# Six loads of short rows against one load of long rows, for gate weights in an attention and expert kernel

## The chip, the cores and the metric

The kernel runs on one core of a Trainium2 chip. The metric is the device time of one execution in microseconds. Each timed run also records its span (first to last instruction, about 1.7 us less than the time) and the mean clock granted to TensorE. Some executions fall into a slower state: 310 to 315 us at a granted clock of 0.977 to 0.984. They are left out of every comparison here; each median below is that of the fast runs. Each kernel has one profiled execution per run, so the times within a profile are those of one execution.

## The reference, cut to what matters

```python
# a gated recurrence over 768 steps gives x, 3072 rows of 384; then a dense mixture of 4 experts:
p = domain_probs / (domain_probs.sum(-1, keepdims=True) + 1e-09)   # (3072, 4), float32
for e in range(4):
    h = np.maximum(x @ w1[e], 0.0)          # 384 -> 1024
    out += p[:, e:e + 1] * (h @ w2[e])      # 1024 -> 384
```

A row of `domain_probs` is four numbers, 16 bytes. The whole array is 48 KB, beside 36 MB that the kernel moves in all.

## The kernel before

The sequence is cut into 6 chunks of 128 steps. Chunk c's attention is computed while chunk c-1's experts run. A small list scheduler in the kernel, with assumed costs for every step, fixes the order of all engines at build time; the parts below are `Op`s of that plan. `rooms` are buffers, and `ps_m` holds the four PSUM banks of the expert products.

```python
pt = const.tile([128, B * C, E], FP32)       # raw probabilities, 384 bytes per partition
pn = const.tile([128, B * C, E], FP32)       # normalised
psm = const.tile([128, B * C, 1], FP32)
w1_sb = wpool.tile([128, E, KD, F], BF16)    # every later tile lies behind these constants
...
def load_w(i, e, which):                     # weights, cast to bf16 on the way, from GpSimd
    ins["w", i] = nc.gpsimd.dma_start(out=w[:, e], in_=r[e])
    if i == 0:
        after(ins["w", 0], ins[0, "k", B - 1])      # not before the last k of chunk 0 has landed
...
def load_p(c):                               # 512 rows of 16 bytes
    nc.sync.dma_start(out=p_dst[:, :, c], in_=p_src[:, :, c])
def probs(c):                                # sum, + 1e-9, reciprocal, product: four small VectorE steps
    ...
def ev_o(c, e, nt, part, cols, eng):         # out += p * (h @ w2), out of PSUM
    pe = pn[:, nt * C + c, e:e + 1]
    ...
# loads of chunk 0, from SyncE, each 192 KB as 1,024 rows of 192 bytes:
for i, x in enumerate("f0 k0 q0 f1 k1 q1 f2 f3 k2 q2 v0 k3 q3 v1 v2 v3".split()):
    add_load(0, x[0], int(x[1]), 1, -1000 + i)
...
for c in range(C):
    pl = P.add(f"ld p{c}", {"DMA": 0.5}, ..., -900 if c == 0 else u0 - 6, lag=2.0)
    pdone.append(P.add(f"probs {c}", {"DVE": 0.8}, ..., u0 + 4, deps=[pl, xdone[c, B - 1]]))
...
for o in done:                               # emission; o.pad filler matmuls keep TensorE busy at the start
    for _ in range(o.pad):
        nc.tensor.matmul(out=spare[:, 0:256], lhsT=busy[:, 0:128], rhs=busy, start=True, stop=True)
    o.emit(o.engine)
```

## Time and profile before

| kernel before | |
|---|---|
| time, median of the first 3 runs | 303.41 us (302.98 to 304.57) |
| profiled execution | 304.22 us, span 302.5 us |
| TensorE busy | 97% |
| first expert matmul to last matmul's end ("the body") | 23.83 to 299.42: 275.59 us |
| last matmul's end to the end of the span ("the end") | 3.10 us |
| the six probability loads, issue to landing | 2.1 to 7.2 us, median 2.7 |

I split the span into three parts throughout: the start up to the first expert matmul (`x @ w1`), the body, and the end. TensorE is the limit in the body; the start is a chain through loads and all engines.

### The profile page before, as it was taken

Reading aid. Unit: us, or ns where it says so; the run is one execution under the profiler, and the core shown is the slowest. Engines: PE = TensorE matmul, PEld = TensorE weight load, DVE = VectorE, ACT = ScalarE, POOL = GpSimd, SP = SyncE. Lnnn points to the kernel's source line nnn. Section 1 sums busy time; section 2 is a strip of 40 time slices with the busy share of each in tenths; the row PEclk is TensorE's granted clock in tenths of the full one; section 3 lists DMA queues with packets and bytes.
Section 4 is the critical chain, followed back from the end, with each engine's and each line's share of the span. In section 5 each row is a group of like instructions: output and inputs, shape, how many; then the busy total and the mean of one; then the engine's idle time right before and its main releaser. Section 6 shows DMA issues by size and latency. Waiting matters only on the chain.

```text
span 302.5 us, 5544 instructions
## 1 busy us (share of the span) xinstructions
PE 294.6 (97%) x2141; PEld 170.9 (56%) x2141; DVE 136.8 (45%) x269; ACT 172.1 (57%) x299; POOL 95.7 (32%) x157
## 2 busy tenths in 40 slices
PE   7898999999999999999999999999999999999995
PEld 5664555566775566556555555555556555555553
DVE  6693002789753574526364426364315253201223
ACT  5766664857776464677455575435566444475440
POOL 4584300407666047332434252622342100000000
PEclk9999999999999999999999999999999999999999
DMA  8999999963995559967799978200422201100003
GB/s 159 206 175 207 208 207 196 218 100 61 216 217 113 113 110 186 179 137 152 141 175 160 220 167 154 50 15 13 115 62 52 48 13 32 66 21 2 0 0 106
DMA packets 137355, 36.10 MB, mean 119 GB/s; under 512 B 128496, under 2 KB 135792, under 8 KB 137328
## 3 DMA queue, kind: packets, MB, share of 16 engines
q1 hardware_dynamic: 131568, 29.45, 49.8%
q0 software_dynamic: 5760, 6.29, 12.5%
q8 instruction: 17, 0.28, 0.4%
q14 instruction: 10, 0.08, 0.1%
HBM read 31.51 MB, written 4.72 MB: 120 GB/s over the span
## 4 chain that ended last, share of the span: by engine, by line
PE 90%; DMA 4%; DVE 3%; POOL 1%; ACT 1%; issue 1%; DVEq 0%; ACTq 0%; POOLq 0%
PE ps_m L356 40%; PE ps_m L344 40%; DMA w_sb<-in_moe_w_dram 3%; PE ps_t L300 2%; PE ps_t L255 1%; PE ps_t L315 1%; PE ps_t L321 1%; PE ps_t L311 1%; POOL qk L276 1%; DMA f<-in_f_logit_dram 1%; DVE qk L276 1%; PE ps_m L569 1%; PE ps_t L285 1%; DVE AT L304 0%; POOL Sf L335 0%
## 5 line engine op out<-in xcount | busy, mean ns | idle before, releaser
L344 PE MATMUL ps_m<-xT,w_sb 128*128 128x512 bf16 (+1 forms) x624 | 153.1, 363 | 1.3 <-DMA w_sb<-in_moe_w_dram 0.9
L356 PE MATMUL ps_m<-w_sb,h 128*128 128x384 bf16 x776 | 153.2, 324 | 0.0
L352 ACT ACTIVATE h<-ps_m 128x512 bf16<-128x512 f32 (+1 forms) x169 | 97.3, 577 | 98.0 <-PE ps_m L344 93.8
L356 PEld LDWEIGHTS <-h 128*128 128x128 bf16 x776 | 73.5, 98 | 58.6
L363 DVE SCALAR_TENSOR_TENSOR o<-ps_m,pn,o 128x384 f32<-128x384 f32 (+1 forms) x73 | 44.6, 611 | 107.2 <-PE ps_m L356 101.3
L344 PEld LDWEIGHTS <-w_sb 128*128 128x128 bf16 x624 | 59.5, 98 | 47.7 <-DMA w_sb<-in_moe_w_dram 1.1
L276 POOL TENSOR_TENSOR qk<-q,e 128x384 bf16<-128x384 f32 x18 | 21.6, 1204 | 64.3 <-ACT e L262 63.9
L350 DVE TENSOR_SCALAR h<-ps_m 128x512 bf16<-128x512 f32 (+1 forms) x39 | 21.9, 578 | 27.1 <-PE ps_m L344 24.2
L304 DVE TENSOR_TENSOR AT<-ps_t,mask 128x512 bf16<-128x512 f32 x48 | 30.2, 682 | 7.4 <-PE ps_t L300 7.4
L335 POOL TENSOR_TENSOR Sf<-Sf,egs 48x192 f32<-48x192 f32 x40 | 20.7, 517 | 39.9 <-DVE Sf L328 37.8
L276 POOL TENSOR_TENSOR qk<-k,e 128x384 bf16<-128x384 f32 x21 | 22.2, 1059 | 20.2 <-ACT e L264 12.9
L262 ACT ACTIVATE e<-ps_t 128x384 f32<-128x384 f32 x24 | 20.7, 864 | 4.8 <-PE ps_t L255 2.6
L328 DVE TENSOR_TENSOR Sf<-Sf,ps_t 48x192 f32<-48x192 f32 x40 | 14.0, 350 | 10.8 <-PE ps_t L321 10.0
L365 ACT ACTIVATE o<-ps_m,pn 128x384 f32<-128x384 f32 x20 | 11.6, 580 | 5.8 <-PE ps_m L356 4.3
L336 POOL CAST sb<-Sf 48x192 bf16<-48x192 f32 x40 | 13.6, 339 | 2.6
L569 PE MATMUL ps_m<-busy 128*128 128x256 bf16 x69 | 12.8, 333 | 1.3 <-DVE busy L140 1.3
L218 POOL CAST vb<-v 128x384 bf16<-128x384 f32 x18 | 9.7, 558 | 11.9 <-DMA v<-in_v_dram 9.7
L264 ACT ACTIVATE e<-ps_t 128x384 f32<-128x384 f32 x24 | 13.0, 541 | 0.0
L247 ACT ACTIVATE ex<-f 128x768 f32<-128x768 f32 (+1 forms) x14 | 10.5, 748 | 3.2 <-DMA f<-in_f_logit_dram 3.2
L315 PE MATMUL ps_t<-vb,AT 128*128 128x48 bf16 x192 | 11.4, 184 | 0.7 <-DVE vb L218 0.7
L315 PEld LDWEIGHTS <-AT 128*128 128x128 bf16 x192 | 9.8, 97 | 2.5 <-issue 0.9
L251 ACT ACTIVATE gp<-ex 128x768 bf16<-128x768 f32 (+1 forms) x14 | 10.5, 751 | 0.4
(50 smaller groups left out, 141.7 us busy)
## 6 DMA issues: line engine op xcount, KB each, us to landing
w_sb<-in_moe_w_dram POOLq DMA_DIRECT2D x8, 768.0 KB, 19.2
out_dram<-o SPq DMA_DIRECT2D x23, 192.0 KB, 2.1
f<-in_f_logit_dram SPq DMA_DIRECT2D x10, 384.0 KB, 4.2
k<-in_k_dram SPq DMA_DIRECT2D x10, 384.0 KB, 5.3
q<-in_q_dram SPq DMA_DIRECT2D x10, 384.0 KB, 5.3
v<-in_v_dram SPq DMA_DIRECT2D x10, 384.0 KB, 5.5
f<-in_f_logit_dram SPq DMA_DIRECT2D x4, 192.0 KB, 3.8
k<-in_k_dram SPq DMA_DIRECT2D x4, 192.0 KB, 4.0
```

What stands on the lines that cost most here:

```text
L262: nc.scalar.activation(out=e[:, 0].rearrange("t (d h) -> t h d", d=D), in_=cs[:, 0:HD].rearrange("t (i r d) -> t r i d", r=2, d=D), func=A ...
L276: engines[eng].tensor_tensor(out=tl("qk", c, b)[:, j, :, 0:D].rearrange("t (i r) d -> t i r d", r=2), in0=tl("qk"[j], c, b // 2)[:, hh(b), ...
L304: nc.vector.tensor_tensor(out=tl("AT", c, b)[:, r].rearrange("s i t -> s (i t)"), in0=tl("A", c, b, r).rearrange("s i t -> s (i t)"), in1= ...
L315: nc.tensor.matmul(out=y[:, h * D:(h + 1) * D], lhsT=AT[:, r, i, :], rhs=vb[:, h, :], start=(c == 0), stop=True, skip_group_check=True)
L328: nc.vector.tensor_tensor(out=Sf[rows, b], in0=Sf[rows, b], in1=KV[rows, :, r, :], op=ALU.add)
L335: nc.gpsimd.tensor_tensor(out=Sf[rows, b], in0=Sf[rows, b], in1=eg, op=ALU.mult)
L344: nc.tensor.matmul(out=tl("hp", c, e, fc, n0)[:, n0:n1], lhsT=w1_sb[:, e, kk, fc * 128:(fc + 1) * 128], rhs=tl("xT", c)[:, kk, n0:n1], sta ...
L350: nc.vector.tensor_relu(out=dst, in_=src)
L352: nc.scalar.activation(out=dst, in_=src, func=AF.Relu)
L356: nc.tensor.matmul(out=tl("op", c, e, nt, part)[:, cols], lhsT=tl("h", c, e)[:, fc, nt * T:(nt + 1) * T], rhs=w2_sb[:, e, fc, cols], start ...
L363: nc.vector.scalar_tensor_tensor(out=o, in0=op, scalar=pe, in1=o, op0=ALU.mult, op1=ALU.add)
L569: nc.tensor.matmul(out=spare[:, 0:256], lhsT=busy[:, 0:128], rhs=busy, start=True, stop=True)
```

## The change

The intent is to take six small loads off SyncE's queue, to keep the first from standing in front of the weights, to normalise once, and so to free VectorE. The array is read as 24 rows of 2,048 bytes; each expert's column of it is turned by TensorE into PSUM.

```diff
-    pt = const.tile([128, B * C, E], FP32)
-    pn = const.tile([128, B * C, E], FP32)
-    psm = const.tile([128, B * C, 1], FP32)
+    NR = B * C
+    praw = const.tile([NR, T, E], FP32)
+    ident32 = const.tile([NR, NR], FP32)
+    nc.vector.tensor_copy(out=ident32, in_=ident[0:NR, 0:NR])
+    pn = const.tile([T, E, NR], FP32)
+    psm = const.tile([T, NR], FP32)
...
-        nc.sync.dma_start(out=p_dst[:, :, c], in_=p_src[:, :, c])
+    def load_p():
+        nc.scalar.dma_start(out=praw, in_=moe_domain_probs.rearrange("(r p) e -> r p e", p=T))
+    def pe_pp():
+        for e in range(E):
+            nc.tensor.transpose(out=tl("pp")[:, e], in_=praw[:, :, e], identity=ident32)
+    def probs():   # the same four steps, once, for all 24 columns
...
-        pe = pn[:, nt * C + c, e:e + 1]
+        pe = pn[:, e, nt * C + c:nt * C + c + 1]
...
-            at = P.add(f"at {c}.{bs[-1]}", {"PE": 0.4 if len(bs) == 1 else 0.66}, ...
+            at = P.add(f"at {c}.{bs[-1]}", {"PE": 0.43 if len(bs) == 1 else 0.66}, ...
...
+    pl = P.add("ld p", {"ACT": 0.1}, lambda e: load_p(), -1100, lag=3.0)
+    pp = P.add("pp", {"PE": 0.6}, lambda e: pe_pp(), -1, deps=[pl], takes=[("ps_m", "pp")], lag=0.2)
+    pdone = P.add("probs", {"DVE": 0.9}, lambda e: probs(), 4, deps=[pp, xdone[0, B - 1]], frees=[("ps_m", "pp")])
```

## The prediction

> **What bounds the kernel now.** I read the page first (busy shares, the 40 slices, the chain that ended last), then the chain in order of time, then the timeline of the two places where the chain leaves the matmuls, and last the windows around the first probability load.
>
> ```profile
> span 302.5 us, 5544 instructions
> PE 294.6 (97%) x2141; PEld 170.9 (56%) x2141; DVE 136.8 (45%) x269; ACT 172.1 (57%) x299; POOL 95.7 (32%) x157
> PE   7898999999999999999999999999999999999995
> PE 90%; DMA 4%; DVE 3%; POOL 1%; ACT 1%; issue 1%; DVEq 0%; ACTq 0%; POOLq 0%
> ```
>
> TensorE is busy 97% of the span, and 90% of the chain that ended last is TensorE. I checked that this is real work and not waiting counted as busy: the matmuls from the first expert layer at 23.83 us to the end at 299.4 us stream 646,464 columns in all, and 512 columns take 0.215 us from start to start in an undisturbed stretch (the three at 24.49, 24.71 and 24.92 us). That is 271 us of 275.5. So after the start at most some 4 to 6 us can be won by any means, and the gaps above 0.25 us add up to 1.25 us only, all between 71 and 83 us. The probabilities are a side branch: six small loads, and four tiny VectorE operations for each of six chunks. They can matter only where they touch the chain of waits. I find two such places.
>
> The first is the start. The chain, in order of time, with start, length and what:
>
> ```profile
> 5.60 2.58 PE ps_m L569 x12
> 13.58 1.31 POOL qk L276
> 14.89 8.90 DMA w_sb<-in_moe_w_dram
> 23.83 1.47 PE ps_m L344 x6
> ```
>
> The expert work cannot start before the first weight load lands. That load is issued at 14.89 us, when GpSimd has finished its third product. TensorE's filler matmuls (L569, which keep it warm) stand on that chain, 12 of them at 5.6 us. The first probability load is issued at 14.79 us, just ahead of the weights. In the timeline and in the windows of that stretch (the last columns of the windows are clock, DMA share and GB/s):
>
> ```profile
> 14.79 0.93 SPq L237 DMA_DIRECT2D pt<-in_moe_domain_probs_dram  x1
> 14.89 6.83 POOL L229 DMA_DIRECT2D w_sb<-in_moe_w_dram  x8
> ...
> 17.00:17.50 0.50, 0.50 (x12) 0.39 (x12) 0.50 (x1) 0.47 (x2) 0.50 (x2) 1.00 1.21 88
> 17.50:18.00 0.50, 0.49 (x13) 0.35 (x8) 0.50 (x3) 0.00 (x0) 0.50 (x1) 1.00 0.92 55
> ...
> 23.00:24.00 1.00, 0.17 (x1) 0.11 (x2) 0.00 (x0) 0.00 (x0) 0.00 (x0) 1.00 1.16 219
> ```
>
> Where the 512 packets of 16 B lie among the first weight packets the rate is 88 and 55 GB/s, against 219 later. TensorE waits for the weights at the end:
>
> ```profile
> 23.83 0.98 PEld L344 LDWEIGHTS <-w_sb 128*128 128x128 bf16 x6 [1.13 <-DMA w_sb<-in_moe_w_dram]
> ```
>
> The second place is chunk 1's normalisation, which stands in VectorE's order directly ahead of two evictions that TensorE waits for:
>
> ```profile
> 81.95 0.20 DVE L244 TENSOR_TENSOR pn<-pt,psm 128x16 f32<-128x16 f32 x1
> 82.18 1.14 DVE L367 TENSOR_SCALAR o<-ps_m,pn 128x384 f32<-128x384 f32 x2
> 82.86 3.37 PE L344 MATMUL ps_m<-xT,w_sb 128*128 128x256 bf16 x27 [0.34 <-DVE o L367]
> ```
>
> **What the Trainium skill says.** DMA: Bandwidth & Descriptors, section "Why small descriptors are slow (HBM only)": each packet pays a fixed overhead, and each operation carries 32 bytes of descriptor beside its data. The trace agrees in kind: alone, a probability load moves its 8 KB in about half a microsecond of packets (a median of 2.7 us from issue to landing), a rate near 16 GB/s. Same page, "Queues, rings and completion order": SP and ACT each own one row on the same 16 DMA engines, which take turns between rows by packet. So moving the load to ACT's queue saves it a place in SP's line but gives no bandwidth of its own; the kernel before issues nothing from ACT, so its trace cannot show that. TensorE: Matmul & The Clock Gate, "What's actually happening" and "Part 4: PE-mode transpose": the array runs at half rate until about 3.4 us of sustained activity, and transposes do not count as activity in the same way. The trace agrees with the first: the 12 fillers at 5.46 us take 2.72 us (0.22 us apart), five at 20.09 us take 0.71 us (0.11 us apart), so the array was cold until after 8 us. No line here shows the second.
>
> **The change part by part.** *Removed loads.* Six issues of about 0.6 us on SyncE's queue (0.93 for the first) and 3,072 packets of 16 B. Five of them land amid work whose waits do not end on them, so they are worth nothing. The first lies ahead of the weights: 512 packets at 9 to 22 ns each over 16 engines is 0.3 to 0.7 us of DMA time, call it 0.5. The rest of the slow stretch I take to be the weight queue's own beginning, because the first 2,048 B packets take 800 ns against 173 later; that is a choice. The weights can win at most 0.8 us for TensorE: the last transposed input is copied from 22.47 for 0.48 us, and the last fillers end at 22.98, so matmuls cannot start before about 23.05.
>
> *Added load.* One issue from ACT right behind the table load (0.80 + 1.28 us = 2.1 us). ACT waits for f until 3.71 us, so the issue is hidden. 24 rows of 2,048 B are 48 KB, at 200 GB/s 0.24 us of DMA, shared with the loads of q, k and f. With 0.6 us of issue and the 2.1 to 2.7 us of the small loads it lands at about 4.8 us.
>
> *Added transposes.* They stand on TensorE behind the first cumulative sums (L255 and L258, which end at 5.4 to 5.6 us), so a landing at 4.8 is in time. The build order shows four 128x24 transposes in place of three of the 12 fillers, 69 becoming 66. Three cold fillers are 3 x 0.22 = 0.65 us. There is no fp32 matmul in this trace; the cold bf16 transposes stand about 0.12 us apart (four in 0.63 us, less the 0.27 us that one takes), and I allow one to one and a half of that each, 0.5 to 0.7 us: even. At most 0.4 us could be won, because the transposes of q at 7.98 us wait for the fillers and not for q, ready at 7.38.
>
> *VectorE.* Six times (0.17 + 0.33 + 0.18 + 0.18 us), 5.1 us in all, become one set over 96 elements in PSUM at 22 us, where VectorE then has nothing to do until 25.5. By the slope of the PSUM copies (0.56 us for 384 elements) it is about 0.25 + 0.19 + 0.20 + 0.26 = 0.9 us. VectorE's total falls by some 4 us. Only chunk 1's 0.83 us (81.32 to 82.15) lies on the path. TensorE's lost time at 82.9 and 83.4 us is 0.51 + 0.20 us above the streaming rate, so that is the most that this can return.
>
> *Moved work.* The plan of the kernel is made anew. From the first expert layer on the order of all engines differs, other buffers of the matmul room are taken, VectorE takes an eviction of QK in chunk 1 and gives others to ACT, and the 0.47 and 0.27 us that TensorE loses at 71.2 and 73.3 us, waiting for products on VectorE, may grow or go. I count this as 0, plus or minus 0.8 us.
>
> Sum: start -0.4 (weights -0.5, fillers 0, a little for a later warm-up +0.1), chunk 1 -0.5, the rest 0: -0.9 us before discount. As new orders tend to bring a wait of their own, I take 0.7, so 303.4 - 0.7 = 302.7 us.
>
> **The rivals.** (1) *The new load becomes a wait.* TensorE takes its instructions in order, so if the probabilities land at 7 us instead of 4.8, everything behind stops. For it: the six loads ahead fill the DMA (214 GB/s from 5 to 10 us), and the first small load took 7.2 us to land behind others. Against: it is on another row of the same engines, and is only 24 packets. It would also keep the array cold for another 3.4 us. This costs 0.5 to 1.5 us at the start: 303.5 to 304.5. (2) *The weights do not come earlier*, because the 55 GB/s are their own start. Then only chunk 1 is left: about 302.9 to 303.1. (3) *The new order loses more than it wins* between 66 and 90 us, the one stretch where VectorE, ACT and GpSimd are all busy over 75% (10.78, 9.91 and 9.96 of 13 us in the window of 70 to 83): plus 1 us, about 304. (4) *All goes well*: start -0.8, chunk 1 -0.7, the waits at 71 and 73 us gone, -0.7: 301.2.
>
> **Range and chances.** The rivals run from 301.2 to 304.5 with most weight on small gains; three runs of the kernel before already span 302.98 to 304.57. 8 in 10: 301.3 to 304.0. A change of 2% is 6.1 us. To be that much faster, all loss after the start would have to vanish; to be slower by that, a wait longer than any in this trace would have to appear. Faster 0.01, within 2% 0.98, slower 0.01.
>
> **What would show it.** Right: first expert matmul between 23.1 and 23.6 us; the windows at 17 to 18 us well above 88 and 55 GB/s; 66 fillers; no wait of TensorE for the probabilities; one set of small operations on VectorE, its total near 132.7 us; the wait near 82.9 us gone; TensorE busy 97% still. Wrong: a TensorE idle ended by the probability load near 5.4 us, fillers still 0.22 us apart after 10 us, the first expert matmul at or after 23.9 us, or new gaps above 0.25 us that add up to more than 1.25 us.

## The result, and the profile after

The changed kernel took 303.90 us in the median of 5 fast runs (303.51 to 304.42; a sixth run was slow, 314.16), the kernel before 303.55 us in 6 runs beside it. The ratio is 1.0012, with a 95% interval of 0.9989 to 1.0035. Ratios here are the mean time of one kernel's fast runs over that of the other's of the same rounds, so they are not quite the ratio of the medians quoted. The time lies inside the predicted range, at its upper edge, on the other side of "before" than predicted.

From the page of the changed kernel, the span, the busy shares and the chain that ended last:

```profile
span 302.7 us, 5502 instructions
PE 291.0 (96%) x2111; PEld 169.8 (56%) x2142; DVE 131.4 (43%) x248; ACT 172.4 (57%) x300; POOL 96.5 (32%) x158
PE 90%; SPq 4%; DMA 2%; issue 1%; DVE 1%; ACT 0%; DVEq 0%
```

VectorE fell by 5.4 us, as intended. TensorE's 3.6 us less are not a saving: 31 matmul records are missing from this trace (593 of 624 on the line of the first expert layer). What is new is 4% of the chain on SyncE's queue, the issues of the first loads. The same part of the chain, in order of time (start, length, what), where before the weights stood:

```profile
14.57 6.62 DMA v<-in_v_dram
...
22.54 0.34 PE ps_t L344 x3
...
24.64 0.38 PE ps_m L348
```

The start is now bound by the last v load: it landed at 21.19 us, against 17.93 before. The timeline adds what waited for loads (idle time and its cause in brackets):

```profile
0.83 0.63 ACTq L238 DMA_DIRECT2D praw<-in_moe_domain_probs_dram  x1
...
5.44 0.66 PE L242 MATMUL ps_m<-ident,praw 24*128 24x24 f32 x4
...
15.23 6.78 POOL L232 DMA_DIRECT2D w_sb<-in_moe_w_dram  x8 [0.46 <-DMA k<-in_k_dram]
...
21.21 0.51 ACT L219 CAST vb<-v 128x384 bf16<-128x384 f32 x1 [2.27 <-DMA v<-in_v_dram]
```

The new load did all that was asked of it. It was issued during the table load, its packets were through by 2.2 us, and the four transposes ran at 5.44 us without a wait. But k and v came late, so GpSimd issued the weights 0.34 us later than before. And v, still in the queue when the weights began, was overtaken: after 18.0 us its last 104 rows of 192 bytes were served beside weight packets of 2,048 bytes, one now and then, until 20.65 us.

| profiled execution | start | body | end | span |
|---|---|---|---|---|
| before | 23.83 | 275.59 | 3.10 | 302.52 |
| after | 24.64 | 274.59 | 3.48 | 302.71 |

So a gain of 1.0 us in the body stands against losses of 0.8 at the start and 0.38 at the end. The experiments are about where each of these comes from.

### The profile page after: what moved, and what is told of

It reads as the page before. It is cut to its first block, busy times and chain, and to the rows that moved or that the text cites. A ratio compares the mean times of both kernels' runs of the same rounds, so it can differ in the third digit from the quotient of the medians.

```text
span 302.7 us, 5502 instructions
## 1 busy us (share of the span) xinstructions
PE 291.0 (96%) x2111; PEld 169.8 (56%) x2142; DVE 131.4 (43%) x248; ACT 172.4 (57%) x300; POOL 96.5 (32%) x158
## 4 chain that ended last, share of the span: by engine, by line
PE 90%; SPq 4%; DMA 2%; issue 1%; DVE 1%; ACT 0%; DVEq 0%
PE ps_m L360 41%; PE ps_m L348 40%; SPq L225 4%; DMA v<-in_v_dram 2%; PE ps_t L304 2%; PE ps_t L319 1%; PE ps_t L325 1%; PE ps_t L315 1%; PE ps_t L259 1%; PE ps_t L289 1%; DVE qk L280 1%; PE ps_t L344 0%; DVE yb L221 0%; PE ps_m L573 0%; ACT xT L219 0%
## 5 line engine op out<-in xcount | busy, mean ns | idle before, releaser
L348 PE MATMUL ps_m<-xT,w_sb 128*128 128x512 bf16 (+1 forms) x593 | 149.9, 362 | 1.5 <-issue 0.2
L354 DVE TENSOR_SCALAR h<-ps_m 128x512 bf16<-128x512 f32 (+1 forms) x37 | 20.9, 581 | 28.3 <-PE ps_m L348 27.0
L266 ACT ACTIVATE e<-ps_t 128x384 f32<-128x384 f32 x24 | 20.8, 865 | 5.2 <-PE ps_t L259 3.2
L369 ACT ACTIVATE o<-ps_m,pn 128x384 f32<-128x384 f32 x22 | 12.8, 581 | 4.8 <-PE ps_m L360 4.1
L573 PE MATMUL ps_m<-busy 128*128 128x256 bf16 x66 | 11.0, 304 | 1.3 <-DVE busy L140 1.3
```

The source lines that it names most:

```text
L266: nc.scalar.activation(out=e[:, 0].rearrange("t (d h) -> t h d", d=D), in_=cs[:, 0:HD].rearrange("t (i r d) -> t r i d", r=2, d=D), func=A ...
L348: nc.tensor.matmul(out=tl("hp", c, e, fc, n0)[:, n0:n1], lhsT=w1_sb[:, e, kk, fc * 128:(fc + 1) * 128], rhs=tl("xT", c)[:, kk, n0:n1], sta ...
L354: nc.vector.tensor_relu(out=dst, in_=src)
```

## The experiments

Twelve runs were made, on three chips. All results were correct.

### The changed kernel again

No edit.

> The changed kernel, unchanged. In its first profile the first expert matmul came at 24.64 us and the last v load landed at 21.19 us, against 23.83 and 17.93 in the kernel before. Theory A (order of transfers): the late v is built in, because the first weight load is now issued only 0.66 us after that v load's issue (0.99 before) and overtakes it; then the last v lands after 20 us again and the first expert matmul stands at 24.2 us or later, time within 0.3% of before. Theory B (an accident of memory speed in that one execution, whose 192 B packets took 21 to 24 ns between 4 and 8 us): v lands near 18 us, first expert matmul at 23.0 to 23.6, and the median is 0.2 to 0.4% below that of before.

Measured: 303.89 us (303.59 to 303.93, 5 runs), before 303.23 us, ratio 1.0022 (1.0009 to 1.0034): a small loss, clear of noise. Start 23.48, body 274.93, end 3.46 us. The last v landed at 18.88 us. Neither theory held. The late v was not built in, since a delay of one microsecond was gone; but the slow packets were no accident either: between 4 and 8 us they took 21.9 ns again, where the kernel before has 15.4.

### The weights held back

```diff
-            after(ins["w", 0], ins[0, "k", B - 1])
+            after(ins["w", 0], ins[0, "q", B - 1])
```

> Changed kernel, except that the first weight load waits for the last q load instead of the last k load, about 1 us later. Theory A: v keeps its place, lands at 18.0 to 18.5 us, the transposed input is ready near 23.0, weights land at 23.4 to 24.0, the first expert matmul follows at once; the start is 0.5 to 1 us earlier than in the changed kernel and the time 0.2 to 0.3% below it. Theory B: weights only come later, the start and the time lose 0.3 to 0.7 us against the changed kernel.

Measured: 304.66 us, ratio 1.0051 (1.0038 to 1.0063), 0.77 us worse than the changed kernel of the same call. Start 23.61, body 275.84. Weights issued at 16.16 instead of 15.19 us landed only 0.12 us later, at 23.56, and v landed at 19.76 us. The loss lies later. From the waits of TensorE, with total, count and longest:

```profile
PE ps_t L259 <- ACT gp L255: 2.2, 4, 1.1
```

and in its timeline, the cause of that wait:

```profile
53.70 0.84 ACT L251 ACTIVATE ex<-f 128x768 f32<-128x768 f32 x1 [1.85 <-DMA f<-in_f_logit_dram]
```

The f of chunk 1 is held behind the sixth weight load, so weights that come later make chunk 1 late. The first theory fell: the order of transfers around the weights was not the thing to repair.

### The new order alone

```diff
# kernel before
-{"PE": 0.4 if len(bs) == 1 else 0.66}
+{"PE": 0.43 if len(bs) == 1 else 0.66}
```

> Kernel before, with nothing of the change but the cost 0.43 in place of 0.40 that the plan assumes for one product of Q and K; this reorders the body of the program and touches no probability. If the change's gain of about 1.0 us between the first expert matmul and the last comes from the new order, a good part of it (0.5 us or more) is seen here; if it comes from the normalisation taken off VectorE, this takes the 275.6 us of before, within 0.3 us. The start is as in before, 23.8 us.

Measured: body 274.65 us, 0.94 less than in the kernel before, with six loads and six normalisations as before. Time 302.63 us in the median (302.49 to 304.32), the lowest of all; ratio 0.9995 (0.9973 to 1.0018), because one run of 304.32 widens the interval. A gain of that size is thus to be had from a new order alone. It is not quite the order of the changed kernel, whose plan has other steps: here VectorE forms both of its products of chunk 1 from k (at 56.76 us), there one from q and one from k (at 57.04 and 59.16 us). The changed kernel's own order without its probabilities was not run. The two gaps at 71 and 73 us (0.47 and 0.27) are gone; the wait that the prediction wanted to remove is still there, now at 81.32 us:

```profile
80.65 1.14 DVE L367 TENSOR_SCALAR o<-ps_m,pn 128x384 f32<-128x384 f32 x2
81.32 1.95 PE L344 MATMUL ps_m<-xT,w_sb 128*128 128x256 bf16 x14 [0.34 <-DVE o L367]
```

### The change in the old order

The plan of the kernel before is kept, with its steps for the probabilities left empty; the long-row load, the transposes (for three fillers) and the one normalisation are put in at emission.

```diff
+    P.slot["ps_m", "pp"] = 2
+    load_p()
     for o in done:
+        if o.name == "tpq 0.0":
+            pe_pp()
+            o.pad -= 3
```

> The change without its new order: plan and order of the kernel before, six loads and six normalisations taken out, one load from ACT, the four transposes in place of three fillers and one normalisation put in. If the probabilities themselves are worth what the prediction said, the wait of 0.5 us near 82.9 us is gone and the body is 275.1 us or less, and the first weights land 0.5 us or more earlier after their issue. If the order is what counts, the body stays at 275.4 to 275.8 us. Time: 302.6 by the first, 303.2 to 303.6 by the second.

Measured: 304.59 us, ratio 1.0047 (1.0034 to 1.0061). Start 23.81, body 275.47, end 3.47 us. This is the test of the step that promised most. From its timeline:

```profile
81.33 1.14 DVE L370 TENSOR_SCALAR o<-ps_m,pn 128x384 f32<-128x384 f32 x2
...
83.59 0.55 ACT L267 ACTIVATE e<-ps_t 128x384 f32<-128x384 f32 x1
84.02 0.94 ACT L355 ACTIVATE h<-ps_m 128x256 bf16<-128x256 f32 x3
...
84.46 1.80 PE L347 MATMUL ps_m<-xT,w_sb 128*128 128x256 bf16 x15 [0.61 <-ACT h L355]
```

Without chunk 1's normalisation the evictions start 0.85 us earlier (81.33 for 82.18), and TensorE no longer waits at 82.9 us. It waits at 84.46 us instead, for ACT, which is busy with four exponentials from 81.9 to 84.1 us and evicts nothing meanwhile. The lost time is 0.78 us, where it was 0.51 + 0.20. The wait changed its owner and kept its size, so the normalisation was worth nothing here: the body of 275.47 us is that of the old order with it (275.40 to 275.59).

In the changed kernel, with its own order, TensorE has no wait near 81 to 83 us, as predicted, but one that the kernel before and the run with the new order alone do not have there:

```profile
58.77 0.65 PE L289 MATMUL ps_t<-ident,qk 128*112 128x128 bf16 x8 [0.42 <-DVE qk L280]
```

### The kernel before again, one look

No edit.

> Kernel before, unchanged, for a second profile of it: its first one fell on an execution of 304.22 us, near the top of its range. Expected: time 302.7 to 303.5, last matmul to the end of the span 3.1 us again, body 275.3 to 275.8 us, 192 B packets of 15 to 16 ns between 4 and 8 us, first expert matmul at 23.0 to 23.2 us in place of 23.83.

Measured: 306.81 us, state unknown, with v landing at 21.47 and the first expert matmul at 25.16 us. It missed what was expected of it and says little; it shows that the kernel before, too, can have its last v overtaken. Its granted clock was 0.50 from 24.3 to 27.6 us, so that its first expert matmuls ran at half rate; its body of 276.84 us is no measure of the kernel. Its end was 3.10 us and its packets took 15.4 ns.

### An added load from ACT, at the start and late

```diff
# kernel before; e5 issues it when chunk 3's first expert product is emitted
+    extra = const.tile([B * C, T, E], FP32)
+    nc.scalar.dma_start(out=extra, in_=moe_domain_probs.rearrange("(r p) e -> r p e", p=T))
```

> Kernel before with one thing added: the 48 KB load of 24 long rows from ACT's queue at the start, into a tile that nothing reads. Every engine's order is else that of before. If the use of ACT's queue itself costs (theory C): the end after the last matmul is 3.45 us instead of 3.1, the 192 B packets between 4 and 8 us take 21 ns or more instead of 15.4, and the time is 0.8 to 1.4 us (0.3 to 0.45%) above before. If the cost of the old-order run lies in the transposes or the normalisation (theory D): the time stays within 0.3 us of before.

> The same added load, but from ACT in the middle of the program (chunk 3's first expert layer, near 160 us), when the first loads are long done. Theory C with a cost at the end that depends only on the queue being used: end 3.45 us again, but packets of 15.4 ns at the start and a time only 0.3 to 0.5 us above before. If the end is 3.1 us here, the queue's cost at the end depends on when it is used.

Measured, beside 303.47 us before: at the start 303.61 us, ratio 1.0008 (0.9994 to 1.0021), end 3.03 us, packets 15.6 ns; late 303.71 us, ratio 1.0015 (1.0001 to 1.0029), end 3.04, packets 15.4 ns. Neither the slow packets nor the longer end came with ACT's queue. What the queue itself costs is at most a few tenths. Theory C fell. Theory D, which would put the old-order run's loss on the transposes or the normalisation, was left for now; what follows accounts for that loss without it.

### The long rows from SyncE

```diff
# changed kernel
-        nc.scalar.dma_start(out=praw, ...
+        nc.sync.dma_start(out=praw, ...          # emitted behind the last v load; transposes behind the last copy of x
```

> The changed kernel with its order, but the one long-row load issued by SyncE behind the last v load, where the first short-row load stood before, and the four transposes at the end of the start instead of at 5.4 us. Theory C: end 3.1 us, packets of 15.4 ns, first expert matmul at 22.9 to 23.3, body 274.6 to 275.0; time 302.3 to 302.9, below both kernels. If ACT's queue is not to blame: within 0.2 us of the changed kernel, 303.7 to 304.1.

Measured: 304.04 us, ratio 1.002 (1.0007 to 1.0034): no better. Packets 20.8 ns, end 3.49 us, with nothing issued from ACT. In its profiled execution TensorE was granted half its clock from 8 to 14 us, so its start of 23.86 us says little.

By now the slow packets and the long end stood in every kernel that carries the change's constants and one load for six, whatever queue it used, and in none of the others. So I compared where the built programs put their tiles (byte address in a partition, and that modulo 64):

```
            before           after
f (0, 1)    101888   0       103648   32
k (0, 1)    104960   0       106720   32
q (0, 1)    108032   0       109792   32
f (2, 3)    117280  32       119040    0
v (0, 1)    136768   0       138528   32
```

The constants grew from 864 to 2,624 bytes, by 1,760, which is 27.5 times 64. Every tile behind them changed its place relative to 64 bytes.

### Thirty-two bytes, both ways

```diff
# e7: changed kernel; e8: kernel before
+    const.tile([128, 8], FP32, name="pad32")      # behind psm, never used
```

> Changed kernel plus one unused tile of 32 bytes per partition, so that all later tiles start where they did in the kernel before, counted modulo 64 bytes (the change made the constants 1,760 bytes larger, which is 27.5 times 64, so f, k, q and v moved from multiples of 64 to 32 beyond one). No instruction changes. Theory E (alignment of the loads' 192-byte rows): packets between 4 and 8 us take 15 to 16 ns instead of 21 to 23, the last k load lands near 14.4 instead of 14.9 us, the first expert matmul comes 0.3 us or more earlier, time 0.3 to 0.6 us below the changed kernel. If not E: packets of 21 ns or more, and the changed kernel's time, 303.9.

> The other way round: kernel before plus the same unused tile of 32 bytes, nothing else. Theory E: packets between 4 and 8 us take 21 to 23 ns instead of 15.4, the last k load lands 0.3 to 0.6 us later, time 0.3 to 0.7 us above before (0.1 to 0.25%). If not E: no difference.

Measured, beside 303.52 us before: the padded changed kernel took 303.11 us (303.01 to 303.24), ratio 0.9983 (0.9958 to 1.0008), start 23.01, packets 15.3 ns. The padded kernel before took 304.40 us, ratio 1.003 (1.0006 to 1.0054), packets 21.2 ns. No instruction differs from the unpadded kernels, so it is shown that the place of the tiles sets the packets' time, and, for the kernel before, that it costs time. The padded and the unpadded changed kernel did not run in one call. The windows from 4 to 8 us, last columns clock, DMA share and GB/s (a share above 1 means that packets overlap on an engine); first before, then before with the pad:

```profile
4.00:8.00 4.00, 3.58 (x20) 2.52 (x19) 1.91 (x3) 2.93 (x7) 1.10 (x1) 1.00 1.11 220
```

```profile
4.00:8.00 4.00, 3.50 (x19) 2.44 (x18) 1.91 (x3) 2.95 (x7) 1.02 (x1) 1.00 1.36 195
```

and then the changed kernel, and the changed kernel with the pad:

```profile
4.00:8.00 4.00, 3.01 (x24) 2.17 (x23) 1.93 (x4) 3.09 (x7) 1.19 (x1) 1.00 1.40 190
```

```profile
4.00:8.00 4.00, 3.65 (x21) 2.69 (x20) 1.94 (x4) 2.97 (x7) 1.17 (x1) 1.00 1.08 214
```

The rate follows the pad and not the kernel. The Trainium skill has a rule that would explain it, in DMA: Bandwidth & Descriptors, section "How a descriptor splits into AXI transactions": a transaction starts at a multiple of 256 bytes, and a row that does not start there pays for the bytes below its start, in beats of 32 bytes. Row h of these tiles starts 192h bytes behind the tile's. From a multiple of 64 the four possible starts cost 6, 12, 10 and 8 beats, 9 in the mean; from 32 beyond one they cost 7, 13, 11 and 9, so 10. This is an estimate from that page's rule, applied to the destination. It says 11% more, and 220 against 195 GB/s is 13%, 214 against 190 also 13%. It does not say why the packets take 38% longer (21.2 for 15.4 ns), and no run tested other shifts, so the mechanism is argued and not shown. The cost is not at the start alone: in the profile of the padded kernel before, 0.36 us of the body were lost too, where chunk 1's q landed at 57.02 us instead of 55.91. I had read the page for the size of rows and not for where they start.

### Six long-row loads, for the end

```diff
# changed kernel with the pad
+        for r in range(0, NR, 4):
+            nc.scalar.dma_start(out=praw[r:r + 4], in_=moe_domain_probs.rearrange("(r p) e -> r p e", p=T)[r:r + 4])
```

> Changed kernel plus the 32-byte tile, and its one load from ACT cut into six of four long rows each, so that the number of loads is again that of before. Theory F (the end): after the last store SyncE waits for the other DMA semaphores one by one at 0.06 us each; loads take those semaphores in turn, and with five loads fewer the last store fell on one that is waited for early. Then here the last matmul to the end of the span takes 3.0 to 3.1 us instead of 3.47, and the time is 0.3 to 0.4 us below the run with the tile alone. If not F: 3.47 us again and no gain.

Measured: end 3.11 us, as theory F has it. The waits of SyncE in the last microseconds, with total, count and longest, of the kernel before, of the changed one, and of this run:

```profile
SPq L599 <- DMA out_dram<-o: 0.8, 2, 0.6
```

```profile
SPq L603 <- DMA out_dram<-o: 1.2, 2, 1.0
```

```profile
SPq L605 <- DMA out_dram<-o: 0.9, 2, 0.6
```

And the instructions of SyncE on the program's last line after the last store had landed, before and after:

```profile
L599 SPq EVENT_SEMAPHORE  x4: 17/22/28, 301.5 to 302.5; - x4
```

```profile
L603 SPq EVENT_SEMAPHORE  x9: 17/28/28, 301.4 to 302.6; - x9
```

At the end SyncE waits for the DMA semaphores one after the other, 0.06 us apart. In the kernel before most of these waits are done while the last store is still under way; in the changed one five more come after it: 5 x 0.06 = 0.3 us of the 0.38. What puts a store on this or that semaphore is the number of DMAs issued before it: the last store signals 109 in the kernel before, 103 in the changed one, with five loads fewer, and 110 with one added load (e4), which SyncE reaches last. Six loads for one bring back the old turn. One added load (e4, e5) gave 3.03 us.

The time was 303.71 us, not the gain expected but 0.6 us above the run with the pad alone. From its timeline:

```profile
0.83 3.41 ACTq L240 DMA_DIRECT2D praw<-in_moe_domain_probs_dram  x6
4.29 0.52 ACT L253 ACTIVATE ex<-f 128x384 f32<-128x384 f32 x1 [2.21 <-DMA praw<-in_moe_domain_probs_dram]
...
5.15 0.37 SPq L226 DMA_DIRECT2D k<-in_k_dram  x1
```

The six issues stood ahead of ACT's first step until 4.29 us, where it came at 3.71 us in the kernel before. An issue took 0.25 to 0.54 us, but the fifth also waited 1.2 us, until the first f had landed at 3.62 us. SyncE's queue waited as well, as it does not in the kernel before:

```profile
SPq L226 <- DMA k<-in_k_dram: 1.2, 1, 1.2
```

The cause is again the semaphores that the loads take in turn. With six more loads in flight, ACT's fifth load had come round to the semaphore of the first f (101) and SyncE's second k load to that of the first k (103), and each waited until that load had landed. The second k load was issued at 5.15 us, against 3.57 in the kernel before. The start was 24.10 us. My cure for the end cost more at the start than it gave.

### All load tiles aligned

As the run before, and the `egs` tiles made 64 bytes wide, so that f and k of the second pair of batches are aligned too.

> As the run before it (tile and six loads), and the small tiles for the last gates are padded to 64 bytes, so that f and k of the second pair of batches, which were 32 beyond a multiple of 64 in the kernel before and in the tile-only run, are aligned as well. Theory E: packets stay near 15 to 16 ns from 8 to 14 us too (17 to 20 before), the last v lands before 17.8 us, first expert matmul at 22.9 to 23.2 us, its floor from the transposes and copies; time 302.2 to 302.8, below both kernels. If alignment matters only for the first tiles: equal to the run before it.

Measured: 303.40 us (302.55 to 304.17), ratio 0.9993 (0.9966 to 1.002), start 23.36, end 3.11 us. Between 8 and 14 us the rate was 224 GB/s against 207 in the run before it and 203 in the kernel before, which may be the alignment; but the packets took 17.0 ns, not 15 to 16, and no less than in e5 without it (17.0), and the time was not below that of the pad alone. The six loads still weigh on it: SyncE's second k load waited 1.4 us, and TensorE for the probabilities:

```profile
6.71 0.63 PE L244 MATMUL ps_m<-ident,praw 24*128 24x24 f32 x4 [0.76 <-DMA praw<-in_moe_domain_probs_dram]
```

In its profile the granted clock was 0.50 from 8.5 to 11.8 us, so its start says little. No run tried full alignment with one load.

## Why the prediction was right or wrong

The time fell within the range and within 2%. The point, a gain of 0.7 us, was wrong in sign: the repeated comparison gives a loss of 0.2%. By its own steps:

- **TensorE is the limit, little can be won.** Right. The one look at the kernel before aside, no kernel's median left the range from 302.6 to 304.7 us.
- **The new load is in time, so no new wait.** Right, with a slip: ACT issued it at 0.83 us, beside the table load and not behind it. Rival 1 did not happen in the changed kernel; with six loads from ACT it did (0.76 us in the last run).
- **Fillers against transposes, even.** Not told apart. The transposes took 0.66 us, within the 0.5 to 0.7 allowed, but the array warmed up anywhere between 5 and 10 us from execution to execution in both families of kernels, which is more than any filler decides. The later warm-up from the transposes is untested: in the profile after, the fillers right behind them at 6.03 us were already 0.11 us apart, but the array was at full rate before them (the matmul at 5.03 us took 0.32 us, its like in the run with six loads, still cold, 0.48). The prediction also took the page's 3.4 us as agreeing with the trace; the trace shows the two rates only, as TensorE was busy for 3.58 of the 4 us from 4 to 8 us and its first fast filler came at 10.1 us.
- **The first weights come 0.5 us sooner after their issue.** Not shown. The first pair of profiles has 8.90 and 8.10 us, but over all runs it is 7.7 to 8.9 with the short rows and 8.1 to 8.4 with one long load from ACT and the weights not held back. The sign that I had named, a higher rate at 17 to 18 us, was misleading: the rate there was 160 and 201 GB/s, but it was v, which should have been through by then.
- **Chunk 1's normalisation gives 0.5 us.** Wrong; this step failed. The old-order run removed it and got 0.78 us of loss for 0.71. In the changed kernel the named sign came true, the wait near 82.9 us is gone, and yet the body was at best 0.06 us shorter than with a new order alone (274.59 against 274.65); what the normalisation is worth in that order was not measured apart. I had looked at what released TensorE and not at what would be next, though ACT's exponentials stood in the same stretch of the timeline.
- **Moved work, 0 plus or minus 0.8.** The size was off, not the mechanism: a new order alone gave -0.94 us of body in its run. The changed kernel's -0.26 to -1.00 (275.33 us in e6, 275.10 with the pad, 274.59 in the first profile) is about as much or less; part of its spread is a wait of up to 0.58 us near 55 us for chunk 1's gates, in the executions where TensorE gets there before f does.
- **What was not in the sum at all** decided the sign: where the tiles lie, and how the end is waited for. The alignment costs 0.9 us by the medians of e8 and by its ratio (0.003 x 303.5; the interval allows 0.2 to 1.6); the changed kernel with the pad is 0.4% nearer to its kernel before than without (0.9983 against 1.0022, on different chips), some 1.2 us. The end costs 0.36 us.

As a rough account, an estimate from these figures: -0.8 (order) + 0.4 (end) + 0.9 to 1.2 (alignment) + 0 (normalisation) = +0.5 to +0.8 us, and measured were +0.35 and +0.66 between the medians. The terms are from single profiles and overlap, as part of the alignment's cost falls in the body. For the old-order run the last three give +1.3 to +1.6, and +1.36 was measured, which leaves nothing for the transposes (theory D). How far the start's remaining spread, from 23.0 to 24.6 us, is due to the moment of warm-up, to stretches at half clock and to v being overtaken, is left open.

The two lowest medians are those of the kernel before with the other cost in its plan (302.63 us beside 303.23) and of the changed kernel with 32 bytes of padding (303.11 beside 303.52). Neither interval excludes "no difference" against before.

## What to carry to other kernels

A change of data layout also moves every tile that is allocated behind it, and the number of DMAs moves every later one to another semaphore, where it may have to wait for an earlier one; look at both before a difference of some tenths of a per cent is given to the change itself. A wait taken off one engine is worth only the distance to the next engine's wait, so read what else is busy in that stretch. When a scheduler is re-run, test its new order without the change.

## What the Trainium skill lacked or had wrong

- DMA: Bandwidth & Descriptors, "How a descriptor splits into AXI transactions": it agrees with the rates here (11% estimated, 13% measured), but is stated without a measurement, and without saying that it holds for rows written into SBUF. For rows of 192 bytes, 32 bytes of shift took the rate from 220 to 195 GB/s and the mean packet from 15.4 to 21.2 ns. That such a shift can come from an unrelated constant tile is on no page I read.
- No page I read has this part of a program's end (Runtime: NRT & Kernel Launch breaks down what lies around a kernel, not this): SyncE's waits for the DMA semaphores, 0.06 us each, one after another; four or nine of its semaphore instructions after the last store, 3.1 or 3.5 us from the last matmul.
- TensorE: Matmul & The Clock Gate, "Part 4: PE-mode transpose": the remark that transposes do not count as activity in the same way led me to expect a later warm-up. No run here tests it. For the moment of warm-up the same page ("What's actually happening") says ±500 ns, from a free-running window; here, in a start where TensorE also waits, the first filler at full rate came between 5.4 and 10.4 us over the profiles.
- DMA: Bandwidth & Descriptors, "Anatomy of one DMA": it gives about 50 ns for the sequencer's dispatch, for loads issued by GpSimd. How many microseconds an issue occupies ACT's queue I found on no page (among the same page's notes on trn3 stands a count of cycles for earlier chips). Here an issue of 24 rows took 0.63 us and issues of 4 rows 0.25 to 0.54 us.
